# The output product of the first two pairs with seven half-size products; weights' sums made in tile two, operand sums in place

## Chip, cores, metric

The kernel runs on one core of one Trainium2 chip. The metric is the device time of one execution in microseconds.

## What is computed

Chunked attention over 64 tokens, then RMS normalisation and a gated feed-forward network, all in 32-bit floats:

```
attn:  B=8, H=8, S=576, D=64; inside each chunk of 64 tokens
       softmax(q k^T / 8) v
x    = attention output as 4608 rows x 512
xn   = x / sqrt(mean(x*x) + 1e-6) * rms_g
out  = (silu(xn @ w_gate) * (xn @ w_val)) @ w_out
       w_gate, w_val: 512 x 1536;  w_out: 1536 x 512
```

## The kernel before

Tokens go in nine tiles of 512 (`TT`). Tiles 0, 1 and 2 are plain (`PLAIN`): for each of the 12 blocks of 128 hidden channels (`NF`), `gated` makes the up products and the gate, `down` adds to four accumulators in PSUM. The other six tiles are three pairs (`NB`). Operands of matmuls are split in a high part, rounded to the 32-bit matmul format, and a low part, the rest; three matmuls (high-high, high-low, low-high) make one product.

A pair is worked on in two stages. The up stage (`up_pair`, line 736 in `product`) takes six steps i; each multiplies a 2x2 block form by seven products of half size (P1, P5, P6, P2, P3, P7, P4 in `ORD`) instead of eight. What the seven need of x, sums and differences of the blocks, is made ahead by `x_sides` and `x_side` ("sides" below, tiles `xp`); what they need of the weights is read from DRAM (`wsd`, tiles `wr`). The result of step i is a tile `g` with two hidden blocks and two tiles of tokens. Then comes the output stage. In pairs one and two it is plain: `split_g` splits a quarter of a `g` (the cast to the high part on ScalarE in line 838, the low part on VectorE in line 839), `down` (line 557) runs 12 matmuls with that part as the fixed operand and the weight `wo` as the moving one; 24 such calls make the stage, 288 matmuls. Eight accumulators are copied out by `evacuate`.

The last pair's output stage is `last_down` (line 912): it, too, takes seven products. They run over p and, within it, over the six i: 42 steps of six matmuls, with the weight as the fixed operand; the result comes out turned, and the host turns it back. `last_sums` makes two differences of each `g` on VectorE, into `spare` (x, which is free by then) and in place; `split_next` splits the operand two steps ahead and makes two more differences. The parts go in turn to tiles of `gp` ("gh", "gl") and of `att` ("e", "eT"), so a tile is free again four steps later. `last_after` adds the products up on their way out of PSUM and `store` writes them.

The weights of these seven products: P1, P2 and P4 take quarters of `w_out` as they are (`wod`, written in tile one by `save_plain`); P5, P6, P3 and P7 take sums. `out_sides` makes these in twelve portions, three during each of the first two pairs and six during the last: it loads the two parts of four quarters from `wod`, sums them and makes four sums (VectorE, lines 590 and 599), splits (603 and 607) and stores to `wol_`. `last_load` loads them in slots of up to four products (`SLOTS`); `out_load` is the plain loader.

Work other than matmuls is spread by `Steps`: a list of functions for each step number. The attention of the next tiles comes in units (`unit_steps`) of seven functions: load, scores and softmax, sums and turning of the exponents, their way back through DRAM, values and normalisation, turning of x through DRAM, its way back. `UNIT_AT` places them in tile two, where `half` is called twice per block, 24 steps. In a pair, `step` is called after each of the up stage's 42 products and, in the output stage, after each `down`; from step 47 on one function of `x_sides` for the next pair is taken from `made` after each step.

TensorE's instructions run in the order written (`manual_schedule`). For the other engines and for DMA queues a planner chooses the order ahead of time: by priority in the order written, `urgent()` moving a group up, filling an idle engine with whatever is ready; it places tiles in free buffers of their pool. The pools that matter: `wts` (18 large tiles: weights, sides, `g`), `xs` (8), `tmp` (4), `gp` (2 of each), `att` (2 of each); in PSUM `ps_h` (2 banks), `ps_acc` (4), `ps_a` (2).

## Time and profile before

| | |
|---|---|
| median of 3 runs (least, most) | 923.41 us (921.58, 924.09) |
| profiled execution, span | 918.5 us, 17489 instructions |
| TensorE, weight loads | 896.5 us (98%), 735.2 us (80%) |
| VectorE, ScalarE, GpSimd | 566.5 us (62%), 446.8 us (49%), 173.6 us (19%) |
| DMA | 242.84 MB, mean 264 GB/s |

The page names no time of the profiled execution other than its span, from the first to the last instruction; the runs' median stands 4.9 us above it. Engines are called PE (TensorE), PEld (its weight loads), DVE (VectorE), ACT (ScalarE), POOL (GpSimd) and SP (SyncE) in the rows. "L839" is line 839 of the kernel; `gl<-g,gh` names the tile written and the tiles read. A row of the timeline has the start in us from the span's begin, the time it took, engine, line, operation, tiles, shape and the count of merged instructions; brackets hold the idle time of the engine before it and what ended it. A group's row has busy time, mean time of one in ns, and idle time before it. A row of stretches has, for each engine, busy us and number of instructions, then the granted clock, the DMA engines' share and GB/s.

### The profile page before, as it was taken

To read this page: it belongs to the slowest core of one execution; us is meant where nothing else is said; L and a number is where in the kernel's file an instruction comes from. 1 tells how busy PE (TensorE), PEld (TensorE's weight loads), DVE (VectorE), ACT (ScalarE), POOL (GpSimd) and SP (SyncE) were. 2 spreads that over 40 slices of the span, in tenths; PEclk is the share of its full clock that TensorE was granted. 3 is DMA by queue.
4 is the path that set the end of the run, shared out by engine and by line. 5 is a ranking of instruction groups with operands and counts; after the bars stand their busy time and mean duration, and the time that the engine had idled before them with its cause. 6 is when DMAs were issued, how large, how long until landed. Compare 5 with 4: busy or idle time off the path is not lost.

```text
span 918.5 us, 17489 instructions
## 1 busy us (share of the span) xinstructions
PE 896.5 (98%) x6900; PEld 735.2 (80%) x6900; DVE 566.5 (62%) x985; ACT 446.8 (49%) x719; POOL 173.6 (19%) x155
## 2 busy tenths in 40 slices
PE   5799999999999999999999999999999999999998
PEld 4578888888887888888888888888888888888886
DVE  6999975454555646864664735557556545544775
ACT  4988944353447543553444424446434332332452
POOL 0100012243200000233332002323330003432200
PEclk9999999999999999999999999999999999999999
DMA  9798999778876543888798778676987865786901
GB/s 351 282 325 308 366 322 370 246 248 250 290 266 170 165 150 119 319 289 304 239 340 309 302 302 321 227 247 248 335 306 273 338 240 197 279 294 205 343 24 69
DMA packets 101969, 242.84 MB, mean 264 GB/s; under 512 B 9344, under 2 KB 64128, under 8 KB 86912
## 3 DMA queue, kind: packets, MB, share of 16 engines
q1 hardware_dynamic: 100832, 241.21, 74.8%
q8 instruction: 54, 0.88, 0.4%
q10 hardware_dynamic: 1056, 0.52, 0.2%
q14 instruction: 27, 0.22, 0.1%
HBM read 176.69 MB, written 65.01 MB: 263 GB/s over the span
## 4 chain that ended last, share of the span: by engine, by line
PE 90%; ACT 3%; DVE 3%; DMA 2%; issue 1%; SPq 1%; POOL 0%; ACTq 0%; POOLq 0%
PE acc L557 24%; PE ps_b L736 11%; PE ps_c L736 11%; PE ps_a L736 11%; PE ps_g L522 9%; PE ps_v L522 9%; PE ps_d L736 5%; PE ps_o L376 2%; PE ps_s L254 2%; PE ps_b L912 2%; PE ps_c L912 2%; PE ps_a L912 2%; DMA kt<-kT_dram 1%; PE ps_d L912 1%; DMA away_x<-xu 0%
## 5 line engine op out<-in xcount | busy, mean ns | idle before, releaser
L557 PE MATMUL acc<-wo,gh 128*128 128x512 f32 x384 | 118.6, 390 | 0.0
L736 PE MATMUL ps_b<-xp,wr 128*128 128x512 f32 x432 | 104.7, 391 | 0.0
L736 PE MATMUL ps_c<-xp,wr 128*128 128x512 f32 x432 | 104.3, 390 | 0.0
L736 PE MATMUL ps_a<-xp,wr 128*128 128x512 f32 x432 | 103.6, 390 | 0.0
L522 PE MATMUL ps_g<-xh,parts 128*128 128x512 f32 x288 | 96.8, 395 | 0.4 <-ACT xh L489 0.2
L522 PE MATMUL ps_v<-xh,parts 128*128 128x512 f32 x288 | 95.2, 391 | 0.0
L736 PEld LDWEIGHTS ps_a<-xp,wr 128*128 128x128 f32 x432 | 80.9, 188 | 16.9
L736 PEld LDWEIGHTS ps_b<-xp,wr 128*128 128x128 f32 x432 | 80.6, 188 | 17.1
L736 PEld LDWEIGHTS ps_c<-xp,wr 128*128 128x128 f32 x432 | 80.8, 188 | 16.9
L557 PE MATMUL acc<-parts,gh 128*128 128x512 f32 x288 | 90.1, 394 | 0.0
L809 POOL TENSOR_TENSOR g<-u,u 128x512 f32<-128x512 f32 x18 | 23.2, 1289 | 330.7 <-DVE u L805 244.2
L557 PEld LDWEIGHTS acc<-wo,gh 128*128 128x128 f32 x384 | 71.8, 188 | 15.2 <-issue 0.2
L838 ACT CAST gh<-g 128x512 fp32r<-128x512 f32 x64 | 39.8, 622 | 80.3 <-PE acc L557 64.4
L839 DVE TENSOR_TENSOR gl<-g,gh 128x512 fp32r<-128x512 f32 x64 | 45.0, 705 | 54.9 <-ACT gh L838 54.9
L557 PE MATMUL acc<-wo,gl 128*128 128x512 f32 x192 | 75.0, 391 | 0.0
L522 PEld LDWEIGHTS ps_g<-xh,parts 128*128 128x128 f32 x288 | 54.4, 189 | 12.7 <-ACT xh L489 0.6
L522 PEld LDWEIGHTS ps_v<-xh,parts 128*128 128x128 f32 x288 | 54.3, 189 | 11.3
L557 PEld LDWEIGHTS acc<-parts,gh 128*128 128x128 f32 x288 | 53.2, 188 | 11.3
L522 PE MATMUL ps_g<-xl,parts 128*128 128x512 f32 x144 | 56.3, 391 | 0.0
L522 PE MATMUL ps_v<-xl,parts 128*128 128x512 f32 x144 | 56.3, 391 | 0.0
L557 PE MATMUL acc<-parts,gl 128*128 128x512 f32 x144 | 56.1, 390 | 0.0
L544 DVE TENSOR_TENSOR sg<-ps_v,sg 128x512 f32<-128x512 f32 x36 | 24.7, 686 | 49.5 <-PE ps_v L522 37.4
(165 smaller groups left out, 1585.7 us busy)
## 6 DMA issues: line engine op xcount, KB each, us to landing
wr<-wsd SPq DMA_DIRECT2D x63, 1024.0 KB, 9.4
wo<-wod SPq DMA_DIRECT2D x24, 1024.0 KB, 8.7
raw<-w_up_dram SPq DMA_DIRECT2D x12, 1024.0 KB, 9.0
vt<-v_dram SPq DMA_DIRECT2D x18, 512.0 KB, 7.3
wsd<-parts SPq DMA_DIRECT2D x18, 512.0 KB, 7.6
qt<-qT_dram SPq DMA_DIRECT2D x17, 512.0 KB, 5.8
kt<-kT_dram SPq DMA_DIRECT2D x17, 512.0 KB, 5.8
out_dram<-o SPq DMA_DIRECT2D x28, 256.0 KB, 2.3
```

The lines of the kernel that those rows point to most:

```text
L254: nc.tensor.matmul(st["s"][j][c * CH : (c + 1) * CH, pr], st["q"][rows, pr, tok : tok + CH], st["k"][rows, pr, tok : tok + CH], start=True ...
L376: nc.tensor.matmul(st["o"][(2 * c + t) * Q : (2 * c + t + 1) * Q, h * D : (h + 1) * D], eT[c][rows, t, h], vt[rows, c, h], start=True, sto ...
L522: nc.tensor.matmul(ps, a[f][:, cols], b[dt], start=(dt == 0 and i == 0), stop=(dt == NDT - 1 and i == 2),)
L544: nc.vector.tensor_tensor(sg, pv, sg, op=ALU.mult)
L557: nc.tensor.matmul(acc[s], a[:, cols], b, start=(f == 0 and i == 0), stop=(f == NF - 1 and i == 2),)
L736: nc.tensor.matmul(ps, w[:, a, m, cols], xp[:, b, kt], start=start and kt == 0 and i == 0, stop=stop and kt == 1 and i == 2, skip_group_ch ...
L809: nc.gpsimd.tensor_tensor(g[:, 0, 1], kp["u2"], kept[0]["u2"], op=mult)
L838: nc.scalar.copy(gh, src)
L839: nc.vector.tensor_tensor(gl, src, gh.bitcast(F32), op=ALU.subtract)
L912: nc.tensor.matmul(ps[m][INTO[p]], w[:, m, a], parts[c], start=p in FROM and i == 0 and k == 0, stop=p in LAST and i == NPR - 1 and k == 2 ...
```

## The change

The output stage of all three pairs becomes `down_pair`, which is `last_down` with a flag. For the first two pairs:

- the operand sums are made in the `g` tiles themselves, not in x, which holds the next tiles: behind the split for P1 on VectorE, behind those for P5, P6 and P2 on GpSimd;
- every second couple of parts goes to tiles of `xs` and `tmp`, for `att` is in use by attention; the block `c11` goes to `tmp`;
- `then` takes the place of the steps: one step after every second product (six matmuls each), so 21 in the stage; the loads of the next pair's first up weights come eight products before its end.

`out_sides` no longer loads from `wod`: it reads both parts of the output weights from SBUF (`out_parts`), which are there until the end of tile two, and makes all twelve portions in tile two, the five sums on GpSimd. Its work tiles are the two halves of `x2`, not yet in use, and the tile "t1". The host turns the rows of all three pairs.

```
-    def out_sides(i, c):
+    def out_sides(i, c, w):
+        cols = slice(c * P, (c + 1) * P)
+        hi, lo = (
+            out_parts[i][:, n].bitcast(F32).rearrange("p f (h c) -> p (f h) c", c=KH)[:, :, cols]
+            for n in range(2)
+        )
...
-        def load():
...
         def sums():
-            nc.vector.tensor_tensor(w[:, :, 0], w[:, :, 0], w[:, :, 1], op=ALU.add)
+            nc.gpsimd.tensor_tensor(w[:, :, 0], hi, lo, op=ALU.add)
...
-                nc.vector.tensor_tensor(o, one, two, op=op)
+                nc.gpsimd.tensor_tensor(o, one, two, op=op)
...
+        return [sums, parts, store]
...
-    def split_g(src, other=False):
+    def split_g(src, homes):
+        gh, gl = (pool.tile([P, TT], F32R, tag=tag, name=name) for pool, tag, name in homes)
...
-    def last_down(t, gs, wos):
+    def down_pair(t, gs, wos, is_last, then):
...
+        main = (gp, "gh", "gh"), (gp, "gl", "gl")
+        if is_last:
+            other = (att, "e", "e"), (att, "eT", "eT")
+        else:
+            other = (xs, "xs", "gh"), (tmp, "tmp", "gl")
...
-            g, t1 = gs[i], spare(i)
+            g = gs[i]
+            t1 = spare(i) if is_last else g[:, 0, 0]
...
-            split[n] = split_g(src, n % 4 > 1)
+            split[n] = split_g(src, other if n % 4 > 1 else main)
+            less = (nc.vector if is_last or p == P1 else nc.gpsimd).tensor_tensor
             with urgent():
-                if p == P5:
-                    nc.vector.tensor_tensor(t1, g[:, 1, 1], t1, op=ALU.subtract)
+                if p == P1 and not is_last:
+                    less(t1, g[:, 0, 1], t1, op=ALU.subtract)
+                elif p == P5:
+                    less(t1, g[:, 1, 1], t1, op=ALU.subtract)
+                elif p == P6 and not is_last:
+                    less(g[:, 0, 1], g[:, 1, 1], g[:, 0, 1], op=ALU.subtract)
                 elif p == P2:
-                    nc.vector.tensor_tensor(g[:, 1, 0], t1, g[:, 1, 0], op=ALU.subtract)
+                    less(g[:, 1, 0], t1, g[:, 1, 0], op=ALU.subtract)
...
+            spots = [x2[:, n : n + 2].rearrange("p s (a n c) -> p (s a) n c", a=2, n=2) for n in (0, 2)]
+            for f in range(NF):
+                if f % 3 == 2:
+                    w = st.tile([P, 4, 2, P], F32, tag="t1", bufs=1, name="w")
+                else:
+                    w = spots[f % 3]
+                for k, todo in zip(OUT_STEPS, out_sides(*divmod(f, 2), w)):   # 0, 2, 3
+                    at.setdefault(6 * f // 5 + k, []).append(todo)
...
-        share = NPR // 2 * (1 + last_pair)
-        for n in range(share):
-            for k, f in enumerate(out_sides(*divmod(b * NPR // 2 + n, 2))):
-                at.setdefault(7 * NPR // share * n + SIDE_STEPS[k], []).append(f)
...
-            for j in range(2):
-                split_next(2 * n + j + 1)
-                down(acc, 2 * i + j, *split.pop(2 * n + j), wos[n])
+        def then(n):
+            if last_pair:
+                return
+            if n == 7 * NPR - 8:
+                ring_load_ahead(0)
+            if n % 2:
                 step()
                 if step.n > 46 and made:
                     made.pop(0)()
...
+        down_pair(t, gs, wos, last_pair, then)
```

## The prediction

> **What bounds the kernel now.** I read the spans, the page's busy times and chain, then TensorE's own waits.

> ```profile
> core 0: 918.5 us, clock 1.000
> PE 896.5 (98%) x6900; PEld 735.2 (80%) x6900; DVE 566.5 (62%) x985; ACT 446.8 (49%) x719; POOL 173.6 (19%) x155
> PE 90%; ACT 3%; DVE 3%; DMA 2%; issue 1%; SPq 1%; POOL 0%; ACTq 0%; POOLq 0%
> PE ps_s L254 <- DMA x<-qT_dram: 6.0, 2, 5.4
> PE ps_x L511 <- ACT x L458: 4.5, 2, 3.6
> PE ps_o L376 <- DMA eT<-away_e: 0.8, 2, 0.5
> ```

> The clock is full, the chain is TensorE's for 90%, and the waits of TensorE are those of the start (the first two) and 0.8 us in tile two. So a matmul taken away anywhere later shortens the run by its step, as long as nothing else becomes late. The step is not the duration; TensorE's timeline shows it:

> ```profile
> 479.18 2.88 PE L736 MATMUL ps_b<-xp,wr 128*128 128x512 f32 x12
> 481.90 2.88 PE L736 MATMUL ps_d<-xp,wr 128*128 128x512 f32 x12
> 484.62 0.62 PE L557 MATMUL acc<-wo,gh 128*128 128x512 f32 x2
> 487.43 1.48 PE L376 MATMUL ps_o<-vt,eT 64*32 64x64 f32 x128
> 488.85 0.73 PE L557 MATMUL acc<-wo,gh 128*128 128x512 f32 x2
> 551.72 1.98 PE L736 MATMUL ps_a<-xp,wr 128*128 128x512 f32 x8
> 676.22 0.63 PE L557 MATMUL acc<-wo,gh 128*128 128x512 f32 x2
> 743.34 2.88 PE L736 MATMUL ps_a<-xp,wr 128*128 128x512 f32 x12
> 857.58 0.39 PE L912 MATMUL ps_a<-gh,wo 128*128 128x512 f32 x1
> 914.47 0.39 PE L912 MATMUL ps_d<-gh,wo 128*128 128x512 f32 x1
> ```

> Twelve matmuls step on by 2.72 us (479.18 to 481.90): 0.2267 us each. The output product of pair one lasts from 484.62 to 551.72, 67.1 us; that of pair two 67.1 us (676.22 to 743.34). Each is 288 matmuls x 0.2267 = 65.3 plus 1.7 for the attention values in between. The last pair, already in seven products, lasts 857.58 to 914.70: 252 x 0.2267 = 57.1, without a stall.

> **The sum's first term.** Each pair drops 36 matmuls: 36 x 0.2267 = 8.16 us, 16.3 for two; the stage becomes 58.9 us. A record of 0.39 us would make it 28. [...]

> **What the shorter stage must hold.** Busy times of pairs one, two and three in the output product:

> ```profile
> 484.60:551.70 67.10, 67.10 (x417) 55.22 (x416) 36.57 (x52) 25.35 (x40) 3.33 (x4) 1.00 0.81 308
> 676.20:743.30 67.10, 67.10 (x417) 55.26 (x417) 37.16 (x53) 25.33 (x40) 3.44 (x4) 1.00 0.76 287
> 857.50:914.90 57.40, 57.36 (x254) 47.15 (x252) 40.84 (x63) 27.86 (x46) 3.78 (x3) 1.00 0.30 113
> ```

> The columns after TensorE's two are VectorE, ScalarE, GpSimd. Pair three shows that splitting 42 operands in 57 us keeps up, but there VectorE makes no sides of the next pair's x, and GpSimd is idle (3.8 us). In pairs one and two both change. The rows of the single instructions:

> ```profile
> L838 ACT CAST gh<-g 128x512 fp32r<-128x512 f32 x64 | 39.8, 622 | 80.3 <-PE acc L557 64.4 <-DVE g L792 6.1 <-DVE gl L839 3.7
> L786 DVE TENSOR_TENSOR u<-ps_b,p 128x512 f32<-128x512 f32 x36 | 24.5, 684 | 27.3 <-PE ps_b L736 27.3
> 865.34 0.69 DVE L887 TENSOR_TENSOR x<-g,x 128x512 f32<-128x512 f32 x1
> 865.95 0.69 DVE L839 TENSOR_TENSOR gl<-x,gh 128x512 fp32r<-128x512 f32 x1
> 521.37 1.23 DVE L680 TENSOR_TENSOR xp<-x,xp 128x1024 fp32r<-128x1024 f32 x1
> 522.51 0.69 DVE L839 TENSOR_TENSOR gl<-g,gh 128x512 fp32r<-128x512 f32 x1
> L699 DVE TENSOR_SCALAR x<-x,g_col 128x512 f32<-128x512 f32 x24 | 11.1, 508 | 2.5 <-DMA x<-away_x 2.5
> ```

> VectorE steps on by 0.61 us for 512 columns (865.34 to 865.95) and 1.14 for 1024 (521.37 to 522.51), a scale takes about 0.5.
> - ScalarE: 18 more casts x 0.62 = 11.2, six copies for four: 25.4 to some 38 of 58.9 us. Beside TensorE, cost 0.
> - VectorE: 18 more low parts and 6 subtractions for the first product, 10 additions from PSUM (0.684) for 4 copies, the weights' sums gone. In steps: 42 x 0.61 = 25.6, 3.7, 6.1, sides of x seven plus four times 1.14 = 12.5, scales 2, attention's tail some 3: 53 of 58.9 us. It fits, barely.
> - GpSimd: 18 subtractions in place, six each behind the operands of products two, three and four (P5, P6, P2).
> - SyncE: twelve loads of 1 MB become 18 of 256 KB and 6 of sums; stores stay 8 of 256 KB. It starts them ahead of use; cost 0 (rival three takes that away).
> - PSUM: banks of P1 are the two that the up product freed long before; the first bank that P5 reuses was read by an addition of the up product more than 8 us before. Cost 0.

> **The wait that the change adds.** GpSimd and VectorE hinder each other when both read SBUF alone:

> ```profile
> 785.08 1.29 POOL L815 TENSOR_TENSOR g<-p,p 128x512 f32<-128x512 f32 x1 [1.47 <-ACT p L783]
> 785.63 1.28 DVE L590 TENSOR_TENSOR w<-w 128x512 f32<-128x512 f32 x1 [0.70 <-issue]
> L590 DVE TENSOR_TENSOR w<-w x12: 634/690/1284, 370.6 to 828.5; 128x512 f32<-128x512 f32 x12
> 861.00 2.38 DVE L839 TENSOR_TENSOR gl<-g,gh 128x512 fp32r<-128x512 f32 x2
> 861.22 1.61 POOL L815 TENSOR_TENSOR g<-p,p 128x512 f32<-128x512 f32 x1 [1.47 <-ACT gh L838]
> L815 POOL TENSOR_TENSOR g<-p,p x18: 1283/1290/1606, 382.3 to 861.2; 128x512 f32<-128x512 f32 x18
> 444.13 0.69 DVE L811 TENSOR_TENSOR p<-p,ps_d 128x512 f32<-128x512 f32 x1 [0.53 <-POOL p L799]
> 444.18 1.29 POOL L803 TENSOR_TENSOR g<-p,p 128x512 f32<-128x512 f32 x1
> ```

> At 785.63 VectorE's sum took 1.28 instead of its median 0.69: it ended 0.54 after GpSimd's end at 786.37, that is, it waited for all of it. At 861.22 GpSimd took 1.61 instead of 1.29 (it waited for VectorE's first), and VectorE's second waited for GpSimd: the two took 2.38 where 1.3 is usual. An operand from PSUM (444.13) is not held: 0.69 beside a GpSimd instruction. So low parts and sides take turns with GpSimd's subtractions, 0.61 or 1.14 against 1.29.

> The reserve of a low part comes from pair three:

> ```profile
> 861.85 0.62 ACT L838 CAST e<-x 128x512 fp32r<-128x512 f32 x1 [0.73 <-PE ps_a L912]
> 865.74 0.39 PE L912 MATMUL ps_c<-e,wo 128*128 128x512 f32 x1
> ```

> The cast for product 6 (counted from 0) starts when product 2 frees its tile, its low part could end at 861.85 + 0.62 + 0.7 = 863.2, and TensorE needs it at 865.74: 2.5 us. A product of six matmuls takes 1.36.

> *Splits 6 to 13* have 7 x 1.36 + 0.61 + 2.5 = 12.6 us. They claim 8 x 0.61 = 4.9, GpSimd's six subtractions 6 x 1.29 = 7.7, and the sides P1 and P2 of the next x 2 x 1.14 = 2.3: 14.9, 2.3 us late. The six subtractions of P6 hang only on those behind P1, so most can run before the stage; if two of them fall in here, 2.6 more: 4.9 late. Without the sides: nothing late.
> *Splits 14 to 17* win the reserve back (4 x 0.75 = 3.0).
> *Splits 18 to 25*: again 4.9 + 7.7, and the next pair's second x, of which a call comes after every second product: four calls are two scales of two (2.0 together) and 2 x 1.14, 4.3. That is 16.9 against 12.6: 4.3 late; nothing late if the low parts always go first. I take half, 2.1.
> *Splits 26 to 41*: no GpSimd; what is left of x (seven calls, 8.0), 16 x 0.61 and ten additions (6.1) make 23.9 in 21.8 us; the 2 us spill into the next up product, whose last side, P4, is used six products of 2.72 us, 16 us, after its start. Cost 0.

> So a pair is late by 4.4 us: from 0 (GpSimd hidden) to 4.9 + 4.3 = 9.2.

> **Tile two.** Per weight sum GpSimd gets one 512-column addition (1.29) and four of 128 columns, which no row shows. The nearest rows:

> ```profile
> 247.00:350.00 103.00, 102.25 (x1166) 83.43 (x1165) 55.97 (x119) 54.45 (x78) 4.33 (x8) 1.00 0.62 192
> L443 POOL TENSOR_TENSOR ri<-ss,mhalf 128x1 f32<-128x1 f32 x32 | 19.0, 602 | 150.3 <-DVE ss L441 149.9
> ```

> Between a quarter of 1.29 (0.32) and one column's 0.60; I take 0.4, nearer to the same operation: 2.9 us, twelve times 35 us of a GpSimd that is busy for 4.3 in 103. VectorE gets 12 low parts (8 us on 56), ScalarE 12 casts (7.5 on 54), SyncE 24 stores, 6.3 MB over some 70 us, 90 GB/s on 192. What can become late is the turned attention: its 0.5 us wait for eT is the one stall here, and its chain (sum, scale, turn, two DMAs) now waits for GpSimd up to 1.3 us in each of four units, and its DMAs stand in SyncE's queue behind stores that wait for low parts. 0 to 5 us; I take 1, since only one of the four units waits now.

> **Taken out of the pairs**: weights' loads, sums and casts lie beside a TensorE that did not wait there: gain 0; a loss is excluded, for nothing takes their place outside the stages above.

> **Sum.** 918.5 - 16.3 + 2 x 4.4 + 1 = 912.0 for the span. The page gives no time of its own beside the span; the median of the runs, 923.41, is 4.9 above it, so 916.9.

> **Rivals.**
> *One: GpSimd stays hidden.* The planner issues sides and P6's subtractions in idle spots; splits 6 to 13 without them need 12.6 of 12.6. For it: in pair one sides ran in gaps between splits, and TensorE never waited. Against: 53 of 58.9 us on VectorE leave few gaps. 923.4 - 16.3 = 907.1, with a little lateness up to 911.
> *Two: slower.* P6's subtractions stay behind their splits, so 18 alternations stand in a row. Each is 0.61 + 1.29 = 1.9: 34.2, and the sides in that stretch 2.3 + 4.3: 40.8, against 17 x 1.36 + 3.1 = 26.2. 14.6 late per pair: 923.4 - 16.3 + 29.2 + 1 = 937. It turns slower from (16.3 - 1 + 2.8) / 2 = 9 us late per pair. For it: turns are seen at 861; against: P6's operands are there early and GpSimd is idle then. [...]
> *Three: loads late.*

> ```profile
> wo<-wod SPq DMA_DIRECT2D x18, 256.0 KB, 9.4
> ```

> Part loads take 9.4 us to land; where tiles are scarce (six g, seven sides, three ring tiles of 18) they are asked for only six to eight products ahead, 8.2 to 10.9. At 1.2 us short for eight of the twelve slots: 9.6 per pair instead of 4.4, 927. Against: pair one's loads ran far ahead.
> That the matmuls stay is no rival: pair three runs the code.

> **Numbers.** Forecast 0.48, rival one 0.25, two 0.18, three 0.09. Range 906.5 to 930: it leaves out most of two. The forecast's own range is 911 to 921. Measurement tells 0.3% (2.8 us) from no change: faster, below 920.6, gets rival one (0.25) and 0.45 of the forecast, 0.70; same gets the forecast's rest and 0.10 of two and three in their mild forms, 0.13; slower, above 926.2, what is left of those, 0.17.

> **What would show it.** TensorE's matmuls 72 fewer; stages of pairs one and two 61 to 65 us; TensorE waiting there for low parts, whose records reach 1.3 to 1.9 us beside GpSimd's; in tile two a wait for eT of 1 to 2 us. Stages of 59 us make rival one right, of 70 or more rival two; waits for wo, three. Low parts at 0.69 throughout would refute the turns.

## The result, and the profile after

The median of the changed kernel is 943.94 us (943.12 to 947.17), beside 922.50 us (919.91 to 924.09) for the kernel before on the same chip: a ratio of 1.0247, interval 1.0222 to 1.0271. It is slower. The profiled execution spans 941.7 us (before 918.5), and its mean granted clock is 0.988 (before 1.000).

The page of the changed kernel, the rows for busy time, the chain and the low parts:

```profile
PE 895.4 (95%) x6828; PEld 727.8 (77%) x6828; DVE 621.5 (66%) x985; ACT 467.7 (50%) x759; POOL 277.2 (29%) x251
PE 61%; DVE 12%; DMA 9%; ACT 6%; issue 5%; POOL 5%; SPq 1%; DVEq 0%; ACTq 0%; POOLq 0%
L830 DVE TENSOR_TENSOR gl<-g,gh 128x512 fp32r<-128x512 f32 x100 | 84.9, 882 | 12.5 <-POOL g L795 6.4
```

The 72 matmuls are gone (6900 to 6828). But the chain, TensorE's for 90% before, is TensorE's for 61%: VectorE, DMAs, ScalarE and GpSimd now hold 32% of it. A low part (line 830 now) takes 882 ns in the mean where it took 705.

TensorE's waits of the changed kernel (us in total, times, longest); those of the start are left out:

```profile
PE ps_c L909 <- DVE gl L830: 8.0, 5, 2.5
...
PE ps_g L522 <- ACT sg L540: 3.3, 2, 1.9
PE ps_c L909 <- ACT gh L829: 3.2, 2, 1.6
PE ps_b L728 <- issue: 3.0, 1, 3.0
PE ps_o L376 <- DMA eT<-away_e: 2.3, 1, 2.3
PE ps_d L728 <- DVE xu L390: 1.9, 1, 1.9
...
PE ps_a L909 <- DVE gl L830: 1.3, 2, 0.6
...
PE ps_b L909 <- DVE gl L830: 0.8, 1, 0.8
```

Before, there were 0.8 us for eT and 0.2 for `sg` of these, and no more. Line 909 is the output stage, 728 the up stage, 522 the gate in the plain tiles, 376 the attention's values. Low parts (`gl`) make TensorE wait 10.1 us in all. The stretches of the output stages of pairs one, two and three and of tile two, in the same columns as in the prediction:

```profile
493.30:564.00 70.70, 64.19 (x381) 50.24 (x380) 61.92 (x71) 34.47 (x57) 31.48 (x20) 0.95 0.76 256
695.50:766.60 71.10, 64.01 (x381) 49.95 (x380) 61.74 (x70) 34.14 (x57) 31.40 (x20) 0.95 0.68 228
880.80:941.70 60.90, 57.32 (x253) 47.13 (x252) 41.50 (x63) 27.82 (x46) 3.75 (x3) 0.99 0.31 116
250.00:359.00 109.00, 102.38 (x1156) 82.64 (x1155) 65.61 (x127) 58.64 (x85) 45.23 (x68) 0.98 0.73 232
```

Stages last 70.7 and 71.1 us where they lasted 67.1. VectorE is busy for 61.9 of 70.7 us, much of it waiting inside its instructions for GpSimd (48.1 us in experiment 4, where only GpSimd's 18 subtractions are left out); the granted clock is 0.95. From one stage's first matmul to the next one's:

| stage, us | before | after | predicted |
|---|---|---|---|
| tiles 0 to 2 | 324.75 | 333.58 (+8.8) | +1 |
| up, pair one | 124.72 | 124.57 (-0.2) | 0 |
| output, pair one | 67.10 | 70.73 (+3.6) | -3.8 |
| up, pair two | 124.50 | 131.43 (+6.9) | 0 |
| output, pair two | 67.11 | 71.13 (+4.0) | -3.8 |
| pair three, both stages | 175.13 | 175.13 (0) | 0 |

The changes add up to 23.1 of the 23.2 us between the spans. An output stage without a stall would last 58.8 us, so pairs one and two are 11.9 and 12.3 us late, 24.2 in all, against 16.6 us that the missing matmuls save.

**Where a stage loses its time.** Timeline of the changed kernel, first part of pair one's output stage (it begins at 493.31; line 880 is the subtraction behind P1, 882, 884 and 886 are those behind P5, P6 and P2):

```profile
497.11 1.76 DVE L830 TENSOR_TENSOR gl<-g,gh 128x512 fp32r<-128x512 f32 x1 [3.19 <-POOL g L795]
499.39 1.41 DVE L830 TENSOR_TENSOR gl<-g,gh 128x512 fp32r<-128x512 f32 x1
500.83 1.66 DVE L880 TENSOR_TENSOR g<-g 128x512 f32<-128x512 f32 x1
503.13 1.66 DVE L880 TENSOR_TENSOR g<-g 128x512 f32<-128x512 f32 x1
504.71 1.28 DVE L390 TENSOR_TENSOR xu<-ps_o,rs 128x512 f32<-128x512 f32 x2
505.43 0.63 ACT L440 ACTIVATE eT<-xu 128x512 f32<-128x512 f32 x1 [8.58 <-DVE xu L390]
508.25 0.60 ACT L829 CAST gh<-g 128x512 fp32r<-128x512 f32 x1
508.90 0.50 PE L909 MATMUL ps_c<-gh,wo 128*128 128x512 f32 x1 [1.61 <-ACT gh L829]
512.18 5.61 POOL L882 TENSOR_TENSOR g<-g 128x512 f32<-128x512 f32 x3 [0.63 <-DVE gl L830]
512.63 1.77 DVE L830 TENSOR_TENSOR gl<-g,gh 128x512 fp32r<-128x512 f32 x1
514.32 2.32 DVE L672 TENSOR_TENSOR xp<-x,xp 128x1024 fp32r<-128x1024 f32 x1
516.57 1.77 DVE L830 TENSOR_TENSOR gl<-g,gh 128x512 fp32r<-128x512 f32 x1
```

Two things are to be read here. From 512 on, the turns: three of GpSimd's subtractions take 5.61 us (1.29 each when alone), a low part 1.77, a side of x 2.32, one after the other without a gap. And before, a queue: VectorE first stands for 3.19 us until GpSimd has made the up stage's last `g` (1.95 us in experiment 4), then its instructions, stretched to 1.4 to 1.8, bring the attention's row `xu` (line 390) to VectorE only at 504.71. ScalarE, whose next instruction in order is the square of `xu` (line 440), stands for 8.58 us, and the cast that TensorE needs comes behind the normalisation, at 508.25. TensorE waits for a cast on ScalarE that is idle for want of VectorE.

The worst wait of each stage is in splits 18 to 25 (pair one, then pair two):

```profile
534.79 0.39 PE L909 MATMUL ps_c<-gh,wo 128*128 128x512 f32 x1
537.71 0.80 PE L909 MATMUL ps_c<-gl,wo 128*128 128x512 f32 x1 [2.53 <-DVE gl L830]
538.30 1.05 PE L909 MATMUL ps_c<-gh,wo 128*128 128x512 f32 x2
737.37 0.39 PE L909 MATMUL ps_c<-gh,wo 128*128 128x512 f32 x1
740.30 0.50 PE L909 MATMUL ps_c<-gl,wo 128*128 128x512 f32 x1 [2.54 <-DVE gl L830]
740.64 0.64 PE L909 MATMUL ps_c<-gh,wo 128*128 128x512 f32 x2
```

Two matmuls behind the first wait take 1.05 us, behind the second, equally long, 0.64: after the first, the granted clock is halved. Short stretches of the changed kernel show the clock in the column ahead of the last two:

```profile
508.00:510.27 2.27, 0.52 (x2) 0.21 (x2) 1.82 (x2) 2.27 (x6) 0.00 (x0) 1.00 0.00 0
510.27:513.68 3.41, 3.41 (x8) 2.73 (x9) 3.31 (x3) 2.67 (x5) 2.78 (x2) 0.50 0.95 298
513.68:520.00 6.32, 5.52 (x24) 4.22 (x24) 6.32 (x6) 2.94 (x6) 4.11 (x3) 1.00 1.05 226
537.58:540.99 3.41, 3.28 (x8) 2.60 (x9) 3.41 (x4) 0.47 (x1) 1.22 (x1) 0.50 0.93 267
```

Summed over the steps of pair one's stage, each less the usual 0.2267 us, five waits cost 7.4 us, 15 steps at half clock 3.0, and slower first steps behind waits and the like 1.6: the 12 us. In pair two it is 8.1, 2.9 and 1.3.

### The profile page after: what moved, and what is told of

Read it like the earlier page. It is cut to its first block, busy times and chain, and to the rows that moved or that the text cites. A ratio compares the mean times of both kernels' runs of the same rounds, so it can differ in the third digit from the quotient of the medians.

```text
span 941.7 us, 17504 instructions
## 1 busy us (share of the span) xinstructions
PE 895.4 (95%) x6828; PEld 727.8 (77%) x6828; DVE 621.5 (66%) x985; ACT 467.7 (50%) x759; POOL 277.2 (29%) x251
## 3 DMA queue, kind: packets, MB, share of 16 engines
q1 hardware_dynamic: 96224, 231.77, 70.7%
## 4 chain that ended last, share of the span: by engine, by line
PE 61%; DVE 12%; DMA 9%; ACT 6%; issue 5%; POOL 5%; SPq 1%; DVEq 0%; ACTq 0%; POOLq 0%
PE ps_a L728 9%; PE ps_c L728 9%; PE ps_b L728 9%; PE ps_c L909 5%; PE ps_d L728 5%; PE ps_g L522 4%; PE ps_v L522 4%; PE acc L557 4%; PE ps_b L909 4%; PE ps_d L909 3%; DVE gl L830 2%; DMA away_e<-e 2%; PE ps_a L909 2%; DMA w<-wfd 2%; DMA away_x<-xu 1%
## 5 line engine op out<-in xcount | busy, mean ns | idle before, releaser
L728 PEld LDWEIGHTS ps_a<-xp,wr 128*128 128x128 f32 x432 | 80.9, 188 | 16.9
L830 DVE TENSOR_TENSOR gl<-g,gh 128x512 fp32r<-128x512 f32 x100 | 84.9, 882 | 12.5 <-POOL g L795 6.4
L557 PE MATMUL acc<-parts,gh 128*128 128x512 f32 x288 | 91.2, 398 | 0.0
L829 ACT CAST gh<-g 128x512 fp32r<-128x512 f32 x100 | 59.8, 621 | 45.8 <-PE ps_b L909 10.6
L522 PEld LDWEIGHTS ps_g<-xh,parts 128*128 128x128 f32 x288 | 54.6, 190 | 16.3 <-ACT sg L540 4.1
L557 PEld LDWEIGHTS acc<-parts,gh 128*128 128x128 f32 x288 | 53.9, 191 | 11.5
L791 POOL TENSOR_TENSOR p<-p,p 128x512 f32<-128x512 f32 x36 | 46.9, 1315 | 40.6 <-DVE p L790 20.3
L769 ACT ACTIVATE p<-p 128x512 f32<-128x512 f32 x36 | 22.6, 632 | 71.2 <-POOL p L791 65.3
L557 PE MATMUL acc<-parts,gl 128*128 128x512 f32 x144 | 56.6, 393 | 0.0
L728 PE MATMUL ps_d<-xp,wr 128*128 128x512 f32 x216 | 53.7, 398 | 1.9 <-DVE xu L390 1.9
L630 POOL TENSOR_TENSOR w<-w 128x512 f32<-128x512 f32 x24 | 32.9, 1371 | 75.9 <-DMA w<-wfd 40.8
## 6 DMA issues: line engine op xcount, KB each, us to landing
wo<-wod SPq DMA_DIRECT2D x54, 256.0 KB, 5.1
```

Of the source, the lines that this page charges most:

```text
L522: nc.tensor.matmul(ps, a[f][:, cols], b[dt], start=(dt == 0 and i == 0), stop=(dt == NDT - 1 and i == 2),)
L557: nc.tensor.matmul(acc[s], a[:, cols], b, start=(f == 0 and i == 0), stop=(f == NF - 1 and i == 2),)
L630: nc.gpsimd.tensor_tensor(out, one, two, op=op)
L728: nc.tensor.matmul(ps, w[:, a, m, cols], xp[:, b, kt], start=start and kt == 0 and i == 0, stop=stop and kt == 1 and i == 2, skip_group_ch ...
L769: nc.scalar.activation(t, t if src is None else src, AF.Silu)
L791: nc.gpsimd.tensor_tensor(kp["p5"], kp["p1"], kp["p5"], op=add)
```

## The experiments

Stage times below are of the one profiled execution, in the order plain tiles / output stage one / two; for the changed kernel they are 333.6 / 70.7 / 71.1. The times are medians; the profiled executions of 9 and 11 took 945.7 and 946.4 us, more than theirs, but their plain tiles start at 40.4 and 40.8 us of the span instead of some 35, and the stage times leave that out. Ratios are to the kernel before.

**1. The 18 subtractions on VectorE.**

```
-            less = (nc.vector if is_last or p == P1 else nc.gpsimd).tensor_tensor
+            less = nc.vector.tensor_tensor
```

> The changed kernel with the 18 subtractions behind P5, P6 and P2 of pairs one and two on VectorE instead of GpSimd. Turns theory (GpSimd's instructions on SBUF hold VectorE's low parts, TensorE waits, then runs at half clock): the output stages of pairs one and two fall from 70.7 and 71.1 us to 59 to 63, no stretch of half clock is left in them, low parts are back at 0.69 us; time 920 to 930. Rival, VectorE is simply full there (61.9 us busy of 70.7): 18 x 0.61 = 11 us more on it makes the stages 75 us or more, time above 948.

931.19 us, 1.0111 (1.0094 to 1.0129); stages 335.0 / 66.9 / 66.0. With the same work on the busier VectorE the run is 12.7 us shorter: 9.0 us in the two output stages, 5.4 in pair two's up stage, against 1.4 lost in the tiles. So the turns with GpSimd are a cause. But the stages stay 8.1 and 7.2 us above 58.8, the time is 1 us above the theory's (and far below the rival's), and two stretches of half clock are left in pair one's stage: the turns are not the whole. Part of the rest is not VectorE's either. SyncE now issues two loads of weights (`wo`) behind the stores of the first output quarter (`c`):

```profile
532.83 1.02 SPq L890 DMA_DIRECT2D out_dram<-c  x2
533.90 0.95 SPq L843 DMA_DIRECT2D wo<-wol  x2
540.50 0.47 PE L909 MATMUL ps_c<-gh,wo 128*128 128x512 f32 x1 [2.21 <-DMA wo<-wol]
```

In the changed kernel these loads are issued at 519.47, ahead of the stores at 534.92, and TensorE never waits for them. Here it waits 2.2 us, and 2.5 us in pair two's stage.

**2. The sums of tile two on VectorE.**

```
-                nc.gpsimd.tensor_tensor(o, one, two, op=op)
+                nc.vector.tensor_tensor(o, one, two, op=op)
```

(and the sum ahead of it alike)

> The changed kernel with the weights' sums of tile two on VectorE instead of GpSimd, all else as it is. Turns theory: tile two, whose plain stretch is 8.8 us longer than before (333.6 against 324.8 us), gets back to within 3 us; time 936 to 939. Rival, the stores and SyncE's queue delay the turned attention: the plain stretch stays within 2 us of 333.6, time 942 to 945.

935.50 us, 1.0157 (1.0140 to 1.0174); stages 330.3 / 70.6 / 70.7. The waits of the gate for `sg` are gone, the one for eT is not: the tiles get 3.3 of the 8.8 us back. That is less than the theory had (to within 3 us) and more than the rival. The other 4.4 us of the gain lie in pair two's up stage, which the edit does not touch.

**3. The edits of 1 and 2 together.**

> Both edits: subtractions and weights' sums on VectorE, no GpSimd in the change. Turns theory: the gains add, stages 59 to 63, plain stretch under 328; time 912 to 922, at or below the kernel before. Rival, VectorE full: 948 or more.

923.39 us, 1.0026 (1.0011 to 1.0041); 329.4 / 64.0 / 64.5. The two gains add up (12.7 and 8.4 us, 20.6 together): GpSimd's part in the change costs some 20 us. Stages, tiles and time all lie 1 to 1.5 us above the forecast. Pair two's up stage is still 4.2 us late.

**4. The 18 subtractions left out.**

```
-                elif p == P5:
+                elif p == P5 and is_last:
...
-                elif p == P6 and not is_last:
...
-                elif p == P2:
+                elif p == P2 and is_last:
```

> The changed kernel without the 18 subtractions of pairs one and two (that part of the computation is left out, the products then take operands that are not their own). Turns theory: stages 59 to 60.5 us, no half clock in them, time 918 to 926, as good as or better than with the subtractions on VectorE. Rival, VectorE full without them: the stages stay above 67 us, time above 937.

921.18 us, 0.9999 (0.9981 to 1.0016); 335.9 / 58.8 / 58.8. The stretch of its first output stage:

```profile
495.10:553.88 58.78, 58.78 (x381) 48.54 (x380) 48.13 (x70) 33.93 (x56) 4.57 (x5) 1.00 0.89 305
```

TensorE never waits, at full clock, with VectorE busy for 48.1 of 58.8 us by everything else that the change gives it. So the whole 12 us of a stage hang on these 18 instructions, 1.29 us each on GpSimd and about 0.6 on VectorE. What they do on VectorE shows in ScalarE's rows, first of experiment 1 (stage from 494.33), then of this one (from 495.10):

```profile
504.61 0.63 ACT L440 ACTIVATE eT<-xu 128x512 f32<-128x512 f32 x1 [6.74 <-DVE xu L390]
507.42 0.60 ACT L829 CAST gh<-g 128x512 fp32r<-128x512 f32 x1
```

```profile
502.63 0.63 ACT L440 ACTIVATE eT<-xu 128x512 f32<-128x512 f32 x1 [4.00 <-DVE xu L390]
505.45 0.60 ACT L829 CAST gh<-g 128x512 fp32r<-128x512 f32 x1
```

The cast behind the normalisation starts 14.9 us into the stage with GpSimd's subtractions, 13.1 with VectorE's, 10.4 without; TensorE waits for it 1.61, 1.04 and 0 us. With the subtractions on VectorE some of them run ahead of `xu`, and the same queue on ScalarE holds the cast.

**5. Experiment 3 without the stores of the weights' sums** (other weights are read in their place).

```
-                for k, todo in zip(OUT_STEPS, out_sides(*divmod(f, 2), w)):
+                for k, todo in zip(OUT_STEPS[:2], out_sides(*divmod(f, 2), w)):
```

> The kernel with subtractions and weights' sums on VectorE, without the 24 stores of the weights' sums in tile two; the output stages read other weights in their place (that part of the computation is left out and replaced). Queue theory (what is left of tile two's lateness, 4.6 us, comes from stores that stand ahead of the turned attention's transfers): the plain stretch goes from 329.4 to 326 us or less, the waits for eT shrink to the 0.8 us of before; time 919 to 921. Rival, VectorE's extra instructions lengthen the attention chain: plain stretch 328.5 or more, time 922 to 924.

922.72 us, 1.0013 (1.0001 to 1.0025); 326.6 / 65.7 / 66.9. Of the 4.7 us that the plain tiles are still late in experiment 3, 2.8 are the stores in SyncE's queue. The 1.9 that remain no run takes apart. The waits for eT shrink to 2.0 us in all, not to 0.8; the time is the rival's. The stages lose what the tiles win: their waits for the weights `wo` grow from 1.84 and 1.35 us in experiment 3 to 1.97 and 3.17. The loads stand behind the stores of `c` here as in experiment 1.

**6. Experiment 3 with the first operand sum made in the up stage.**

```
-            t1 = spare(i) if is_last else g[:, 0, 0]
+            t1 = spare(i) if is_last else g[:, 0, 1]
...
+                nc.vector.tensor_tensor(g[:, 0, 1], g[:, 0, 1], g[:, 0, 0], op=ALU.subtract)
```

> Subtractions and weights' sums on VectorE, and of the four operand sums of pairs one and two the first is made in the up stage, where VectorE is about 60% busy (in place of the second block; the sum for P7 is then made from it and the first block). So VectorE does six instructions, 3.7 us, less in each output stage. If VectorE's load sets those stages (64.0 and 64.5 us): 60 to 62 us each, time 917 to 920, below the kernel before. Rival, the stages wait for weights (wo) and for attention's tail on ScalarE, not for VectorE's load: 63 to 65 us, time 922 to 924.

922.83 us, 1.0014 (0.9998 to 1.0030); 329.6 / 66.0 / 64.5. The time is the rival's. Six of VectorE's 24 subtractions moved out of the stage bring it nothing; the waits are for `wo` (2.40 and 2.27) and for low parts (0.4 to 0.8 each). VectorE's sum of work alone is not what is left.

**7. The kernel before with waits of TensorE put in** where it is otherwise never late: in the up stage of the last pair a transpose waits for a row of small copies on ScalarE.

```
+                    nc.scalar.copy(junk, ps[1]["c"][:, :P])
+                    for _ in range(stall):
+                        nc.scalar.copy(junk, junk)
+                pj = bank(ps_a, "ps_j")
+                nc.tensor.transpose(pj[:, :P], junk, ident)
```

> The kernel before, with five waits put into the last pair's up stage: after product P5 of steps 1 to 5 TensorE transposes a block that ScalarE has first copied 4, 7, 9, 11 and 14 times, so it idles for about 1, 2, 3, 3.5 and 4.5 us. Theory (a stall of more than about two thirds of a 3.4 us stretch of a fixed grid halves the clock of the next stretch): no half clock after the first two, 3.4 us of it after the longer ones, steps of 0.43 us in it; the stage grows by the stalls plus 1.4 us for each stretch. Rival, the half clock of the changed kernel has another cause than its stalls: the granted clock stays 1.0 and the stage grows by the stalls alone.

951.39 us, one run. The waits came out longer than planned, at 2.2, 3.5, 3.8, 4.5 and 5.5 us. Stretches ahead of the first and behind it, then in the second, behind it and further on:

```profile
766.00:769.70 3.70, 3.70 (x18) 3.06 (x17) 1.65 (x3) 1.77 (x3) 2.12 (x2) 1.00 0.49 142
772.00:775.40 3.40, 2.98 (x14) 2.47 (x15) 1.39 (x2) 0.85 (x3) 0.00 (x0) 1.00 0.24 77
791.50:795.10 3.60, 0.34 (x2) 0.00 (x0) 1.55 (x5) 3.04 (x10) 0.01 (x1) 1.00 0.08 27
795.75:799.16 3.41, 3.41 (x9) 2.64 (x8) 0.69 (x1) 0.00 (x0) 0.00 (x0) 0.50 0.49 150
799.20:802.00 2.80, 2.80 (x14) 2.30 (x13) 1.29 (x2) 0.54 (x1) 0.00 (x0) 1.00 0.74 204
```

Behind 2.2 us the clock stays at 1.00, behind 3.5 it is 0.50, and so it is behind two longer ones (in the stretches 819.65 to 823.05 and 843.50 to 850.30). The stage takes 143.1 us where it takes 114.2: 20.2 by the waits, 7.4 by 41 steps at half clock, the rest by the transposes themselves. The first wait, from 770.25 on, is cut by a line of the grid into 1.6 and 0.6 us, so it does not test the theory's two thirds: the changed kernel has 2.45 and 2.41 us idle in the 3.41 us ahead of its stretches at 510.27 and 537.58. Waits alone bring the half clock here, in a stage that has nothing of the change; that the change's new instructions do it falls.

**8. The kernel before with tile two's part of the change alone**, sums on GpSimd.

> The kernel before, plain output stages and all, with only the weights' sums moved to tile two as in the change (GpSimd, from SBUF). Theory (tile two's lateness belongs to the move itself): plain stretch 331 to 336 us instead of 324.8, up and output stages as before, time 928 to 934. Rival, it needs the new output stages (the planner's order as a whole): plain stretch under 327, time 920 to 924.

933.29 us, 1.0132 (1.0104 to 1.0161). The plain tiles take 338.8 us, 14.0 more than before; all other stages are as before to 0.2 us (up stages 124.5, output stages 67.1). TensorE's waits there:

```profile
PE ps_o L376 <- DMA eT<-away_e: 5.9, 1, 5.9
...
PE ps_g L522 <- ACT sg L540: 4.1, 2, 2.4
```

The time is as forecast, the plain stretch 2.8 us longer. So tile two's loss belongs to the move and reaches no later stage. Its size is not fixed: with one and the same tile two, experiments 1, 4 and 8 and the changed kernel lose 10.2, 11.2, 14.0 and 8.8 us, by one wait for eT of 4.8, 5.5, 5.9 and 2.3.

**9. Experiment 6 with the stores of the weights' sums and of `c11` on ScalarE's queue.**

```
-                nc.sync.dma_start(slots[:, n : n + 2], w[:, n : n + 2].rearrange("p n a c -> p n (a c)"))
+                nc.scalar.dma_start(slots[:, n : n + 2], w[:, n : n + 2].rearrange("p n a c -> p n (a c)"))
```

> The kernel with subtractions and weights' sums on VectorE and the first operand sum in the up stage, and two kinds of stores issued from ScalarE's queue instead of SyncE's: those of the weights' sums in tile two, and those of the first output quarter (c) in the output stages, behind which the loads of the sums for P3 and P7 stood (issued at 527.6 us, waited for at 531.6). If SyncE's order is what is left: the 2.3 us waits for wo go and the half clock behind them, stages 61 to 63 us, plain stretch 327 or less; time 914 to 918, faster than before. Rival, the loads are late for want of free tiles: stages stay at 64 to 66 us, time 921 to 923.

939.87 us, 1.0191 (1.0172 to 1.0210); 343.7 / 66.5 / 66.9. Both theories missed. A wait of ScalarE:

```profile
ACT L331 <- DMA wol<-x: 6.1, 1, 6.1
```

What ScalarE does in that time is issue four stores:

```profile
281.34 6.02 ACTq L604 DMA_DIRECT2D wol<-x  x4
```

So ScalarE, which the softmax needs, stands still for 6.1 us behind stores, and the tiles take 14 us more than in experiment 6. In the output stages the wait for `wo` went, and one of 2.27 for a low part came in its place: SyncE's order is not what is left there either.

**10. All stores of the first two output stages on ScalarE's queue too.**

```
-            store(m, 1, 0, kp["p1"])
+            store(m, 1, 0, kp["p1"], nc.sync if is_last else nc.scalar)
```

(and two more stores alike)

> As the run before, with all output stores of pairs one and two issued from ScalarE's queue. SyncE's order: the loads of the next pair's up weights also come earlier, the wait in pair two's up stage (1.5 us) goes, another 1 to 2 us less than the run before. Rival, ScalarE stands still while VectorE's additions end and its casts come late: stages 64 us or more.

946.55 us, 1.0269 (1.0240 to 1.0299); 343.2 / 68.6 / 68.9. ScalarE's casts wait for stores (12.1 us in two waits), as the theory that ScalarE would stand had it.

**11. Experiment 9 with half of the weights' sums in pair one's up stage, read from DRAM.**

```
-            for f in range(NF):
+            for f in range(NF // 2):
...
+        if b == 0:
+            for n in range(NPR):
+                for k, f in enumerate(out_sides_read(*divmod(NPR + n, 2))):
+                    at.setdefault(7 * n + SIDE_STEPS[k], []).append(f)
```

> As e9, with half of the weights' sums in tile two, at half the pace, and the other six in pair one's up stage, read back from DRAM as in the kernel before. If tile two's lateness goes with the number of sums there: plain stretch 325 to 326.5 us, pair one's up stage as before (124.5), time 1 to 3 us below e9. Rival, one late transfer of the turned attention makes it, whatever the number: plain stretch as in e9.

936.55 us, 1.0188 (1.0135 to 1.0241); 335.1 / 65.4 / 66.5. The plain stretch lies between the two forecasts: the tiles win 8.7 us of the 14 back. Pair one's up stage loses 10.7 (135.2); TensorE's waits there add up to 6.7 us, the longest, 3.5 us, for its weights `wr`.

**12 and 13. Experiment 6 with the attention's units 8, then 9 products apart instead of 10**, so that the normalisation lies before the output stage.

```
-                    at.setdefault(4 + 10 * n + PAIR_STEPS[k], []).append(f)
+                    at.setdefault(4 + 8 * n + PAIR_STEPS[k], []).append(f)
...
-                if step.n > 46 and made:
+                if step.n > 42 and made:
```

(nine: `4 + 9 * n` and `> 43`)

> The kernel with subtractions and weights' sums on VectorE and the first operand sum in the up stage, and attention's units in pairs one and two 8 steps apart instead of 10, the sides of x taken from step 43 on instead of 47: attention's tail (normalisation, turning of x) and the first sides leave the output stage for the up stage. If VectorE's and ScalarE's work at the stage's start and middle sets it (64.5 and 66.0 us): 61 to 63 us each, time 914 to 919. Rival, loads of the weights set it: 64 to 66 us, time 921 to 924, or more if the up stage becomes late.

> As the run with units 8 steps apart, but 9 apart (sides of x from step 44 on), so that scores and values fall on different steps. VectorE's other work sets the stage: output stages 61 to 64 us, up stages 124.5 to 127, time 913 to 919, faster than the kernel before. Rival, loads of the weights set it: stages 64 to 66 us, time 920 to 923.

935.10 us, 1.0156 (1.0141 to 1.0170), stages 329.9 / 61.3 / 65.0; and 930.79 us, 1.0097 (1.0075 to 1.0119), 330.2 / 65.5 / 66.8. In both runs the time missed every forecast, but for the rival's remark in 12 that the up stages may become late. Eight apart gives the shortest first output stage of all with subtractions, 61.3: no cast on ScalarE and no `wo` makes TensorE wait there any more, only two low parts (1.5 and 1.8 us). But the up stages pay: 132.7 and 136.0 us, since the scores wait for the bank that the values hold (`ps_s` for `xu`, 6.8 us in 11 waits). Nine apart the up stages lose 4.7 and 5.5, and waits for `wo` (2.48 and 2.21) and low parts are back.

**14. The changed kernel with units nine apart**, the edit of 13 alone.

> The changed kernel, subtractions on GpSimd, with only the units 9 steps apart and the sides of x from step 44 on. Turns theory: the sides that leave the stretch give back 2 to 4 us of the 12 per stage, stages 66 to 69 us, time 936 to 941. Rival, the sides are the main part of the lateness: stages 61 to 63 us, time 925 to 930.

941.09 us, 1.0211 (1.0188 to 1.0235); 335.5 / 66.6 / 67.6. As the turns theory had it, the stages win 4.1 and 3.6, but the up stage of pair one loses 5.8.

No kernel that does all the work is faster than the one before; experiments 3 and 6 come within 0.3% of it.

## Why the prediction was wrong

The forecast of 916.9 us was 27 too low, and its range (to 930) did not hold the time. What was right: 72 matmuls fewer; 58.9 us for a stage without a stall (58.8 in experiment 4); the mechanism, VectorE and GpSimd in turns, with low parts of 1.4 to 1.8 us; P6's subtractions ahead of their place (one at 504.94); no wait for a PSUM bank in the output stages, no cost in pair three; and that without the subtractions VectorE fits (48.1 us in experiment 4, where I took 53). What failed, in order of size:

- **"So a pair is late by 4.4 us"**, with a range from 0 to 9.2. It is late by 11.9 and 12.3. Read from the start of each product in pair one, against experiment 4: 1.3 us late already at product 6; splits 6 to 13 cost 5.7 (I took 2.3, at most 4.9); 14 to 17 cost nothing, as taken; splits 18 to 25 cost 4.5 (I took 2.1, half of 4.3); 0.4 after them. For 18 to 25 a side of x (2.32 at 533.67) stood ahead of the low part that TensorE waited for, so the condition under which I took nothing did not hold. That the upper bound comes out is luck: of the 4.5 us only 2.7 are the wait, and 1.8 the half clock behind it. For 6 to 13 the sum counted VectorE's claims as if only low parts had users; it left out that ScalarE, in order, holds the casts behind a row of the attention that VectorE makes. And the two stretches at half clock behind the waits in pair one's stage (2.45 us idle ahead of 510.27, 2.41 ahead of 537.58) cost some 1.5 us each, 3.0 together, which was in no term. Rival two had the side and the sign right, but not the cause it named: 18 alternations in a row were not needed. The prediction's own turning point, 9 us per pair, is passed by both pairs.
- **"0 to 5 us; I take 1" for tile two.** 8.8, and 14.0 for the move alone. With the sums on VectorE the tiles get 3.3 us back (experiment 2), or 5.6 (experiment 3 beside 1); the stores in SyncE's queue hold the attention (2.8, experiment 5); the remaining 1.9 is not taken apart. The parts need not add up to 8.8, since the loss is not the same with one and the same tile two. I had named both and priced them too low: I judged by the idle time of the engines (GpSimd 4.3 in 103 us), while the one stall of before, 0.5 us for eT, said that this chain has no reserve at all.
- **"a loss is excluded" for the up stages.** Pair two's lost 6.9 us: 1.87 for `xu` at 602, 2.98 at 666 and a stretch at half clock. Experiment 8 shows that it does not come with tile two; in experiment 4, with ideal output stages, it is 5.4. So it comes with the seven-product stage itself. Its size changes from run to run without a pattern that I could find: 1.6, 2.6, 4.2 and 5.4 us in experiments 1 to 4. One part is seen in the trace: at 602 the product `ps_d` waits until VectorE has read the attention's values (`xu`, at 602.33), while in the kernel before it begins at 589.91, ahead of that reading at 590.01; it seems to get the PSUM bank of these values now. Why, and what the wait at 666 is for (tiles of `g` and weights held to the stage's end, stores ahead of loads), no run shows; it stays open.
- The three terms are 15.4, 7.8 and 6.9 us short, 30.1; the 2.2 us between span and median, where 4.9 was taken, and 0.3 in the first term make it 27.

What also stays open: with the subtractions on VectorE the stages keep at 64 to 67 us. Experiments 5, 6, 9 and 13 took one cause away each (stores, six subtractions, SyncE's order, the place of the attention), and each time a wait for `wo` or for a low part was left. The waits for `wo` come by the load behind the stores of `c`: with these stores on another queue they are gone (experiment 9). No run with all the subtractions takes both kinds of wait away.

## What to carry to other kernels

Price an instruction on GpSimd that reads SBUF beside a VectorE with two SBUF operands as the sum of both (here 1.7 us for a subtraction and a low part that take 1.29 and 0.61 alone), and then ask which engine stands in order behind the VectorE instruction so delayed: here ScalarE's casts, behind a row of attention. A stage with 58.8 us of matmuls and 48.1 us of VectorE's work had too little room: 18 instructions more cost 5 to 12 us, part of it because the planner then chose another order of loads. And an engine's idle share says nothing of a chain whose last link already makes TensorE wait 0.5 us.

## What was not expected of the hardware

In the rows from 512.63 to 518.34 the turns alternate, with 1.7 us for a pair of turns of 512 columns (GpSimd's ends at 513.85 and 515.56). At 529.52 they do not: one subtraction on GpSimd takes 3.95 us, and VectorE makes three instructions in the meantime (529.89 to 532.31). And stores issued on ScalarE's queue held ScalarE itself (6.1 us, experiment 9).
